# Gated mix of an S4D convolution and a bilinear GLU: two of each inverse's four stores on GpSimd's queue, a refitted list schedule, and other warm-up work for TensorE

## The chip, the cores and the metric

The kernel runs on one core of one Trainium2 chip. The metric is the device time of one execution in microseconds, as the median of several runs: 584.83 us before the change (three runs, 584.66 to 585.61).

## The reference

Two branches see the same tokens `u` (2048 x 512), and a gate mixes them:

```python
x = A_u
g = _sigmoid((x * gate_w).sum(-1, keepdims=True))
a = _A_ref(x, ...)   # S4D: y = irfft(rfft(u, 4096) * rfft(K, 4096)) + u * D_skip
b = _B_ref(x, ...)   # bilinear GLU: ((x W_gate) * (x W_up)) W_down
return g * a + (1 - g) * b
```

K is the convolution kernel of each of the 512 channels, 2 Re sum over 128 states n of C exp(A dt pos). The GLU is 1792 wide. All is float32.

## The kernel before

**GLU.** The width 1792 is 14 tiles of 128, in four groups (3, 3, 4 and 4 tiles); each group goes over four chunks of 512 tokens. For a tile and a chunk TensorE computes `pg` (gate) and `pu` (up), ScalarE copies `pg` to `h`, VectorE multiplies by `pu`, and the product is split into a high and a low part, `hh` (ScalarE) and `hl` (VectorE), in float32r. All operands of the large matmuls are split in this way, so each product is three matmuls of 128x128 by 128x512: `pg<-xs,wlo` once and `pg<-xs,whi` twice, likewise for `pu`, and `y<-dhi,hl`, `y<-dlo,hh`, `y<-dhi,hh` for the down product. These 2016 matmuls fill most of TensorE's time. At the end of a group ScalarE scales `y` by 1-g into `acc` (three buffers, line 719 on). Group 0 stores `acc` to `out`; the other groups add it there by an accumulating DMA on GpSimd's queue (`out<-acc`).

**Convolution.** It is done as transforms of length 4096 by small matmuls, in four quarters q of 128 channels. VectorE and ScalarE build tables `v` and `x` for 16 blocks of 32 channels; a **k-block** (`kgen`, line 1164) sums over the states with 64 matmuls of 32x64, `k<-v,x`, whose result goes to `kt`. Four blocks make a quarter: `k_first` transforms it and stores it to DRAM as `sk_d`; the tokens' first stage (`u_part`) goes to `su_d` by GpSimd's queue. Then, for each of four parts T of a quarter (`transforms`, line 1459): `m_load` loads `in` from `su_d` and `sk_d` on GpSimd's queue; the **second stage** (`m_second`, line 1278) is 16 matmuls of 32x512, `k<-in,w2s`, evicted by ScalarE to `ev`; `m_product` multiplies the two spectra on VectorE into `y`. After two parts the **inverse** (`m_inverse`, line 1335) is 64 matmuls of 64x128, `k<-y,w3s`. ScalarE evicts its four banks to two tiles `ts`, and four stores (`y_d<-ts`, 256 KB each, lines 1364 to 1375), two for each tile, one for each p, write them to `y_d`. So there are eight inverses and 32 stores. `m_last` reads `y_d` back on SyncE's queue (`in<-y_d`, `x<-y_d`), does the last 16 or 32 matmuls `k<-in,w_t`, applies the gate and adds to `out` by GpSimd's queue. The tiles of `y_d` and `sk_d` in the last quarter are called `ri`, `e`, `x` and `v`, after the tables whose place they take.

**What sets the order.** No line of the code is executed where it stands. Each operation is recorded as a task by `add(engine, us, fn, r, w, rank, after, dma, hold, rows, count, slack)`, and `Work.plan` (line 355) is a list scheduler: it models the time of every task from the costs given, always takes the task that can start first, and among equals the one of lower rank. `Work.run` then issues the tasks in that order, which is fixed for each engine (`InOrder`, line 116; so all instructions of the engines bear line 124). The model's numbers are part of the kernel:

- `us` is the time on the engine, `dma` the size of a transfer in KB at `DMA_RATE`. `Bus` (line 170) serves two queues of transfers, the hardware one and GpSimd's, in proportion to `WEIGHT`. `SENT` is the time from an issue to the transfer's begin, `LANDED` that from its end to the signal, and `SURE` what a reader leaves on top of it.
- `slack` is added to the time at which a task's inputs are ready. `EASE` adds (slack, rank, lateness) to tasks named by engine, tiles and time.
- `fetched` (line 328) holds a task of TensorE back until the instructions are likely to be there: with blocks of 256 instructions that are asked for when TensorE passes a place one block and `LEAD` ahead, `FETCH` us later, and `BEHIND` times as much more as transfers then wait on the bus. `count` is the number of instructions of a task: 256 for a k-block and for an inverse, 64 for a second stage.

**First work.** `first_loads` (line 577) has VectorE write zeros into a tile, and TensorE multiply them (lines 594 to 603) until the first operands have come.

The evictions before the stores are one `act` task for each bank, and the store takes the tile as its input:

```python
for j in range(4):
    st, m = sts[j // 2], j % 2
    evict(q, j, 0.6, ..., [banks[j]], [(st, m)])
```

Of the kernel before, what the change touches and what calls it, by code (L numbers as in the profile page):

```python
# [10 lines left out]
F32 = mybir.dt.float32  # L11
# [3 lines left out]
ALU = mybir.AluOpType  # L15
# [3 lines left out]
P = 128  # L19
# [150 lines left out]
class Bus:  # L170

    WEIGHT = 1.0, 1.58

# [31 lines left out]
class Work:  # L205
# [14 lines left out]

    BLOCK, FIRST, LEAD, FETCH = 256, 193, 64, 5.0
    TABLE = 1.3
    ROOM = {"dve": 0.6, "act": 0.4}
    BEYOND = 60
    BEHIND = 1.05

    EASE = {
        "act:k/e:0.4": (3, 0, 0),
        "act:k/in:0.32": (0.0, 1, 0),
        "act:pb/x:0.31": (0.0, 0, -60),  # L230
        "act:raw/whi:0.62": (0.0, 0, -60),
        "act:t/rt:0.77": (0.0, 0, -200),
        "dve:ev/y:0.6": (3, 0, 0),
        "dve:k/kt:0.42": (0.0, -1, 0),
        "dve:m/v:1.09": (0.0, 0, -20),
        "pool:ts:0.95": (2, 0, 0),
        "sp:in:0.42": (0.0, 1, 0),
        "sp:ri:0.42": (2, 0, 0),
        "sp:w3s/w2s/v:1.3": (0.0, 1, 0),
    }  # L240
    DMA_RATE = 0.33

    SENT = {"sp": 1.15, "act": 1.15, "pool": 1.98}
    LANDED = {"sp": 1.79, "act": 1.79, "pool": 1.5}
    SURE = 2

# [32 lines left out]
    def ready(self, task, d):  # L279

        if d.engine == task.engine == "pe":
            return d.end
        if d.dma and d.start > 20.0 and task.engine in ("pe", "act", "dve"):
            return d.end + self.SURE
        return d.end + self.LAG.get(task.engine, 0.03) + (self.PE_LAG if d.engine == "pe" else 0.0)
# [164 lines left out]
def gated_mix_kernel(  # L450
# [84 lines left out]
    def load(key, src, rank=0):  # L535
        if key in raws:
            return
        t = raws[key] = new("glu", "raw", [P, D], bufs=2)
        add("sp", 0.42, lambda: sp.dma_start(t.t, src), w=[t], dma=256, rank=rank)

# [20 lines left out]
    def rest(hi, lo, src, n):  # L561

        add("act", 0.19 + 0.43 * n, lambda: act.mul(lo.t, hi.t.bitcast(F32), -1.0), r=[hi], w=[lo], rank=0)
        add("pool", 0.95, lambda: pool_q.dma_start(lo.t, src, accum_op=ALU.add), w=[lo], dma=485 * n if n > 1 else 414, rank=0)

# [11 lines left out]
    def first_loads():  # L577
        in_y = lambda shape: new("mid", "y", shape, bufs=2)
        in_ev = lambda shape: new("mid", "ev", shape, bufs=2)
        in_in = lambda shape: new("mid", "in", shape, bufs=2)  # L580
        xsrc = lambda kt: xT[P * kt : P * kt + P, :D]
        w0 = raws["w0"] = in_ev([P, 2, D])
        xt = [load_two(lambda k, n=n: ("x", 0, 0, 2 * n + k), in_y, None, False) for n in range(2)]
        wsrc = wts[0][:, : 2 * D].rearrange("p (k d) -> p k d", k=2)
        for kt in range(KT):

            t, k, ks = xt[kt // 2], kt % 2, slice(P * kt, P * kt + P)
            add("sp", 0.42, lambda t=t, k=k, kt=kt: sp.dma_start(t.t[:, k], xsrc(kt)), w=[(t, k)], dma=256, rank=-1)
# [56 lines left out]
    def tokens(gi, ci, kt):  # L645

        x = xs[kt] = new("glu", "xs", [P, 2, D], F32R, 5)
        if gi:
            add("sp", 0.42, lambda: sp.dma_start(x.t.bitcast(F32), xs_d[ci, kt]), r=[(m_xs, (ci, kt))], w=[x], dma=422, rank=0)
# [3 lines left out]
        add("sp", 0.42, lambda: sp.dma_start(xs_d[ci, kt], x.t.bitcast(F32)), r=[x], w=[(m_xs, (ci, kt))], dma=462, rank=2, after=16.0 + kt if ci == 0 else 0.0)  # L653

# [64 lines left out]
    def evacuate(gi, ci, r, y):  # L719
# [10 lines left out]
        if final:  # L730
            ending.append((r, acc))
        elif gi == 0:
            add("sp", 0.42, lambda: sp.dma_start(ov[:, t, :], acc.t), r=[acc], w=[(m_out, t)], dma=134)
# [82 lines left out]
    def u_part(t):  # L816
        ut = inp([P, 4, D])
        rs = slice(4 * t, 4 * t + 4)
        add("sp", 0.42, lambda: sp.dma_start(ut.t, uv[:, rs, :]), w=[ut], dma=929, after=6.0 + (U_STEP + 1.0) * t)

# [30 lines left out]
        def first(s):  # L851
# [20 lines left out]
            for q in range(KT):  # L872
# [4 lines left out]
                    ),  # L877
                    r=[st], w=[(m_su, (q, n0))], dma=227,
                )
# [92 lines left out]
    def parameters(bs):  # L972
# [7 lines left out]

        add("sp", 0.84, fn, r=m_par, w=[pb], dma=173 * n)
        real = lambda: pb.t[:, 0, :n, 0]
# [178 lines left out]
    def k_block(b, x, v):  # L1161
# [31 lines left out]
    def k_first(q, kt):  # L1193
# [5 lines left out]
        for h in range(2):  # L1199
# [20 lines left out]
            for n0, n, st in sts:  # L1220
                for c in range(4):
# [11 lines left out]
                    ),  # L1233
                    r=[st], w=[(m_sk, (q, m)) for m in range(n0, n0 + n, 8)], dma=41 * n,
                )
# [11 lines left out]

    def w_load(tag, shape, src, kb=327):
        t = new("mid", tag, shape, bufs=2)
        add("sp", 0.42, lambda: sp.dma_start(t.t, src), w=[t], dma=kb, after=150.0)  # L1250
        return t

    def m_load(q, T):
# [11 lines left out]
        for w, (src, m) in enumerate(((su_d, m_su), (sk_d, m_sk))):  # L1265
# [5 lines left out]
                ),  # L1271
                r=[(m, (q, n0)) for n0 in range(0, 32, 8 if w else 4)], w=[(t, (T, w))], dma=655 if w else 585,
            )
# [61 lines left out]
    def m_inverse(q, T0, ys, ws):  # L1335
# [49 lines left out]
    def m_last(q, gs):  # L1385
# [30 lines left out]
        for g, t, n0, n in pieces:  # L1416
# [30 lines left out]
            if n == 1 and n0 == LAST % 2:  # L1447
# [7 lines left out]
                lambda rs=rs, flat=flat: pool_q.dma_start(ov[:, rs[0] : rs[-1] + 1, cs], flat(), accum_op=ALU.add),  # L1455
                r=[*parts, *((m_out, r) for r in rs)], dma=119 * len(rs), rows=rs,
            )
# [113 lines left out]
```

## Time and profile before

| | |
|---|---|
| time, median of 3 runs | 584.83 us (584.66 to 585.61) |
| the profiled execution | 589.44 us, span 587.5 us |
| mean granted clock of TensorE | 0.994 |
| instructions | 14848 |
| DMA | 136.28 MB, 232 GB/s over the span |
| q1, hardware queues (SyncE, ScalarE) | 43.0% of 16 engines' span |
| q0, GpSimd's queue | 39.3% |

One execution was profiled. PE is TensorE's matmuls, PEld its weight loads, which run beside them; DVE is VectorE, ACT ScalarE, POOL GpSimd, SP SyncE. Tiles stand as output <- inputs. In the groups and waits "<-" ahead of a name stands for what ended the idle time; "issue" is time in which the engine waited for nothing that the profile shows. A line of the timeline is start, length, engine, line, operation, tiles, shapes and count, with the wait ahead of it in brackets. A line of the windows is the stretch, its length, the busy time of PE, PEld, DVE, ACT and POOL with their instructions, the granted clock of TensorE (1.00 is full), the busy share of the 16 DMA engines, and GB/s.

### The profile page before, as it was taken

Reading aid. Unit: us, or ns where it says so; the run is one execution under the profiler, and the core shown is the slowest. Engines: PE = TensorE matmul, PEld = TensorE weight load, DVE = VectorE, ACT = ScalarE, POOL = GpSimd, SP = SyncE. Lnnn points to the kernel's source line nnn. Section 1 sums busy time; section 2 is a strip of 40 time slices with the busy share of each in tenths; the row PEclk is TensorE's granted clock in tenths of the full one; section 3 lists DMA queues with packets and bytes.
Section 4 is the critical chain, followed back from the end, with each engine's and each line's share of the span. In section 5 each row is a group of like instructions: output and inputs, shape, how many; then the busy total and the mean of one; then the engine's idle time right before and its main releaser. Section 6 shows DMA issues by size and latency. Waiting matters only on the chain.

```text
span 587.5 us, 14848 instructions
## 1 busy us (share of the span) xinstructions
PE 576.0 (98%) x5996; PEld 435.4 (74%) x5996; DVE 511.7 (87%) x812; ACT 399.1 (68%) x891; POOL 113.3 (19%) x159
## 2 busy tenths in 40 slices
PE   8999999989999999999999999999999999999995
PEld 5777777877887777888767678877778777777774
DVE  5999999977999999999999899996899998346745
ACT  4459978987568779975987585699858553333351
POOL 0003222410201141311122301133221004012011
PEclk9999999998999999999999999999999999999998
DMA  8999959996845798999879958889968259799686
GB/s 282 386 331 351 396 211 362 261 253 161 201 147 88 252 266 190 199 260 285 188 229 241 213 136 299 201 212 195 260 162 246 38 150 280 267 331 239 197 188 125
DMA packets 71687, 136.28 MB, mean 232 GB/s; under 512 B 6852, under 2 KB 35780, under 8 KB 69188
## 3 DMA queue, kind: packets, MB, share of 16 engines
q1 hardware_dynamic: 47668, 87.10, 43.0%
q0 software_dynamic: 23392, 47.98, 39.3%
q8 instruction: 47, 0.77, 0.5%
q10 hardware_dynamic: 560, 0.26, 0.2%
q14 instruction: 20, 0.16, 0.1%
HBM read 80.27 MB, written 55.05 MB: 230 GB/s over the span
## 4 chain that ended last, share of the span: by engine, by line
PE 91%; issue 4%; DMA 2%; POOL 1%; ACT 1%; DVE 1%; DVEq 0%; POOLq 0%; ACTq 0%
PE pg L124 26%; PE pu L124 26%; PE y L124 24%; PE k L124 15%; DMA in<-sk_d 1%; DMA y<-in_xT 1%; DMA sk_d<-ev 1%; POOL out L124 1%; POOL in L124 0%; ACT ev L124 0%; DVE y L124 0%; ACT h L124 0%; ACT xs L124 0%; DVE hl L124 0%; DVE dlo L124 0%
## 5 line engine op out<-in xcount | busy, mean ns | idle before, releaser
L124 PE MATMUL pu<-xs,whi 128*128 128x512 f32 x448 | 140.3, 395 | 0.0
L124 PE MATMUL pg<-xs,whi 128*128 128x512 f32 x448 | 139.4, 392 | 0.5 <-ACT whi L124 0.5
L124 PEld LDWEIGHTS pg<-xs,whi 128*128 128x128 f32 x448 | 84.7, 189 | 19.3 <-ACT whi L124 2.1
L124 PEld LDWEIGHTS pu<-xs,whi 128*128 128x128 f32 x448 | 85.4, 191 | 17.4
L124 PE MATMUL pg<-xs,wlo 128*128 128x512 f32 x224 | 90.6, 405 | 0.1
L124 PE MATMUL y<-dhi,hl 128*128 128x512 f32 x224 | 89.6, 400 | 0.6 <-DVE hl L124 0.6
L124 PE MATMUL pu<-xs,wlo 128*128 128x512 f32 x224 | 90.2, 403 | 0.0
L124 PE MATMUL y<-dlo,hh 128*128 128x512 f32 x224 | 87.4, 390 | 0.0
L124 PE MATMUL y<-dhi,hh 128*128 128x512 f32 x224 | 87.2, 389 | 0.0
L124 POOL DMA_DIRECT2D out<-acc x44 | 38.6, 955 | 167.9 <-ACT acc L124 160.0
L124 ACT COPY ev<-k 128x512 f32<-128x512 f32 x112 | 59.3, 598 | 16.5 <-PE k L124 16.5
L124 ACT CAST hh<-h 128x512 fp32r<-128x512 f32 x56 | 34.8, 622 | 45.8 <-DVE h L124 45.6
L124 DVE TENSOR_TENSOR h<-pu,h 128x512 f32<-128x512 f32 x56 | 38.6, 689 | 30.2 <-PE pu L124 29.7
L124 PEld LDWEIGHTS pu<-xs,wlo 128*128 128x128 f32 x224 | 42.6, 190 | 20.1 <-issue 11.4
L124 ACT ACTIVATE acc<-y,ngate 128x512 f32<-128x512 f32 x62 | 41.7, 685 | 22.7 <-PE y L124 20.5
L124 PEld LDWEIGHTS pg<-xs,wlo 128*128 128x128 f32 x224 | 42.4, 189 | 19.8 <-issue 9.5
L124 ACT COPY h<-pg 128x512 f32<-128x512 f32 x56 | 32.8, 586 | 34.9 <-PE pg L124 33.1
L124 PEld LDWEIGHTS y<-dhi,hl 128*128 128x128 f32 x224 | 42.0, 188 | 19.3 <-issue 7.7
L124 PEld LDWEIGHTS y<-dhi,hh 128*128 128x128 f32 x224 | 42.1, 188 | 9.0
L124 PEld LDWEIGHTS y<-dlo,hh 128*128 128x128 f32 x224 | 42.1, 188 | 7.8
L124 DVE TENSOR_TENSOR hl<-h,hh 128x512 fp32r<-128x512 f32 x56 | 38.4, 685 | 3.2 <-ACT hh L124 3.1
L124 PEld LDWEIGHTS k<-v,x 128*32 128x32 f32 x2048 | 29.4, 110 | 7.6 <-issue 7.2
(130 smaller groups left out, 962.9 us busy)
## 6 DMA issues: line engine op xcount, KB each, us to landing
xs<-xs_d SPq DMA_DIRECT2D x36, 512.0 KB, 6.7
out<-acc POOLq DMA_DIRECT2D x44, 256.0 KB, 6.1
raw<-in_wts SPq DMA_DIRECT2D x33, 256.0 KB, 4.5
xs_d<-xs SPq DMA_DIRECT2D x16, 512.0 KB, 7.6
su_d<-ev POOLq DMA_DIRECT2D x32, 256.0 KB, 7.2
y_d<-ts SPq DMA_DIRECT2D x28, 256.0 KB, 5.8
in<-su_d POOLq DMA_DIRECT2D x12, 512.0 KB, 6.6
sk_d<-ev SPq DMA_DIRECT2D x6, 1024.0 KB, 4.9
```

Of the source, the lines that this page charges most:

```text
L124: got = getattr(self.engine, name)(*args, **kw)
```

## The change

- In `m_inverse` the stores of p = 1, two of the four of each inverse, are issued on GpSimd's queue; only the last inverse (q = 3, T0 = 2) keeps all four on SyncE's. So 14 stores move: SyncE issues 237 DMAs instead of 251, GpSimd 148 instead of 134. A store there is planned with 0.55 us.
- The numbers of the plan are others: `WEIGHT` of GpSimd's queue 1.14 instead of 1.58, `SENT`, `LANDED`, the `dma` sizes of nearly all transfers, `FETCH` 5.5 instead of 5.0 and `BEHIND` 0.8 instead of 1.05, most entries of `EASE`, and `SURE`, which was 2 for three engines and is 3 for TensorE now. A k-block has a slack of 2.0 instead of 1.0.
- In `first_loads` zeros are written to 128x128 instead of 128x512, and TensorE multiplies them three times instead of twice: by 512, 512 and 128 columns, which are the same 128 read again.

```diff
 class Bus:
-    WEIGHT = 1.0, 1.58
+    WEIGHT = 1.0, 1.14
...
-    BLOCK, FIRST, LEAD, FETCH = 256, 193, 64, 5.0
+    BLOCK, FIRST, LEAD, FETCH = 256, 193, 64, 5.5
...
-    BEHIND = 1.05
+    BEHIND = 0.8
...
     EASE = {
-        "act:k/e:0.4": (3, 0, 0),
...
+        "pe:kt/k/ts:2.13": (1, 0, 0),
...
-    SENT = {"sp": 1.15, "act": 1.15, "pool": 1.98}
-    LANDED = {"sp": 1.79, "act": 1.79, "pool": 1.5}
-    SURE = 2
+    SENT = {"sp": 1.39, "act": 1.39, "pool": 1.79}
+    LANDED = {"sp": 1.46, "act": 1.46, "pool": 1.66}
+    SURE = {"pe": 3, "act": 2, "dve": 2}
...
-        if d.dma and d.start > 20.0 and task.engine in ("pe", "act", "dve"):
-            return d.end + self.SURE
+        if d.dma and d.start > 20.0 and task.engine in self.SURE:
+            return d.end + self.SURE[task.engine]
...
-        add("dve", 0.2, lambda: dve.memset(zero.t, 0.0), w=[zero], rank=-1)
+        add("dve", 0.06, lambda: dve.memset(zero.t[:, :P], 0.0), w=[zero], rank=-1)
         def warm():
-            for _ in range(2):
-                pe.matmul(scratch.t, zero.t[:, :P], zero.t, start=True, stop=True)
-        add("pe", 3.4, warm, r=[zero], w=[scratch], rank=-1, count=8)
+            w = zero.t[:, :P]
+            for n in (4, 4, 1):
+                to = scratch.t[:, : n * P].rearrange("p (n d) -> p n d", d=P)
+                rhs = w.unsqueeze(1).broadcast_to([P, n, P])
+                pe.matmul(to, w, rhs, start=True, stop=True)
+        add("pe", 3.85, warm, r=[zero], w=[scratch], rank=-1, count=12)
...
-                r=[acc, (m_out, t)], dma=431, rows=[t],
+                r=[acc, (m_out, t)], dma=442, rows=[t],
...
-        add("pe", 2.05, kgen, r=[x, v], w=[pk], rank=0, hold=[kt], count=256, slack=1.0)
+        add("pe", 2.05, kgen, r=[x, v], w=[pk], rank=0, hold=[kt], count=256, slack=2.0)
...
                 b0 = 32 * (T0 + p) + 16 * h
+                e, us, queue = ("pool", 0.55, pool_q) if p and (q < KT - 1 or not T0) else ("sp", 0.42, sp)
                 add(
-                    "sp", 0.42,
-                    lambda b0=b0, st=st, p=p: sp.dma_start(
+                    e, us,
+                    lambda b0=b0, st=st, p=p, queue=queue: queue.dma_start(
...
-                    r=[st], w=[(m_y, (q, T0 + h, p))], dma=303,
+                    r=[st], w=[(m_y, (q, T0 + h, p))], dma=311,
```

The new numbers give another order on every engine. Three places follow, each row an instruction with its tiles, shape and, where it repeats, its count.

The first place is on TensorE, a little past the middle of its order, before: down products of the GLU stand ahead of these rows, and the second stage of part T = 2 of quarter q = 1 (`k<-in,w2s`) stands among the GLU's matmuls.

```order
L124 MATMUL pg<-xs,wlo 128x512
L124 MATMUL pg<-xs,whi 128x512 x2
L124 MATMUL k<-in,w2s 32x512 x16
L124 MATMUL pu<-xs,wlo 128x512
L124 MATMUL pu<-xs,whi 128x512 x2
```

The same place now: behind the same down products stands the inverse of that quarter's first two parts (`k<-y,w3s`).

```order
L124 MATMUL y<-dlo,hh 128x512
L124 MATMUL y<-dhi,hh 128x512
L124 MATMUL k<-y,w3s 64x128 x64
L124 MATMUL pg<-xs,wlo 128x512
L124 MATMUL pg<-xs,whi 128x512 x2
```

The inverse, which came later, moved ahead of the second stage. Behind it now come 24 matmuls of the GLU, a k-block and 15 more, and only then the second stage.

The second place is on TensorE too, at the first quarter's inverse of parts 0 and 1, at about 230 us in the trace of before. Before, a k-block, 15 matmuls of the GLU, and then a second stage:

```order
L124 MATMUL k<-v,x 32x64 x64
L124 MATMUL pg<-xs,wlo 128x512
L124 MATMUL pg<-xs,whi 128x512 x2
L124 MATMUL pg<-xs,wlo 128x512
L124 MATMUL pg<-xs,whi 128x512 x2
L124 MATMUL pu<-xs,wlo 128x512
L124 MATMUL pu<-xs,whi 128x512 x2
L124 MATMUL pu<-xs,wlo 128x512
L124 MATMUL pu<-xs,whi 128x512 x2
L124 MATMUL pu<-xs,wlo 128x512
L124 MATMUL pu<-xs,whi 128x512 x2
L124 MATMUL k<-in,w2s 32x512 x16
```

Now the same k-block, 12 matmuls of the GLU, and the inverse:

```order
L124 MATMUL k<-v,x 32x64 x64
L124 MATMUL pu<-xs,wlo 128x512
L124 MATMUL pu<-xs,whi 128x512 x2
L124 MATMUL pu<-xs,wlo 128x512
L124 MATMUL pu<-xs,whi 128x512 x2
L124 MATMUL pu<-xs,wlo 128x512
L124 MATMUL pu<-xs,whi 128x512 x2
L124 MATMUL y<-dhi,hl 128x512
L124 MATMUL y<-dlo,hh 128x512
L124 MATMUL y<-dhi,hh 128x512
L124 MATMUL k<-y,w3s 64x128 x64
```

A block of 64 small matmuls (256 instructions in the plan) stands where one of 16 (64 instructions) stood, and three matmuls of the GLU closer to the k-block.

The third place is on GpSimd's queue, a piece of the difference near its middle (- before, + now), with the adds of the GLU (`out<-acc`) and the stores of inverses (`y_d<-ts`):

```order
 L124 DMA in<-sk_d 128x8x128
-L124 DMA out<-acc 128x512 x8
+L124 DMA out<-acc 128x512 x3
+L124 DMA y_d<-ts 64x8x128 x2
+L124 DMA out<-acc 128x512
+L124 DMA y_d<-ts 64x8x128 x2
+L124 DMA out<-acc 128x512 x4
 L124 DMA wlo<-in_wts 128x1024
```

Four stores, two of each of two inverses, stand between the eight adds.

More of the change, by code (lines that the diff above doesn't have):

```diff
@@ L224 @@
     BEYOND = 60
-    BEHIND = 1.05
+    BEHIND = 0.8
     EASE = {
-        "act:k/e:0.4": (3, 0, 0),
-        "act:k/in:0.32": (0.0, 1, 0),
-        "act:pb/x:0.31": (0.0, 0, -60),
+        "act:k/in:0.59": (0.0, 0, -200),
         "act:raw/whi:0.62": (0.0, 0, -60),
         "act:t/rt:0.77": (0.0, 0, -200),
+        "act:v/sq:1.17": (0.0, 0, 20),
         "dve:ev/y:0.6": (3, 0, 0),
[L234 to L238, printed above, removed]
+        "dve:k/in:0.42": (0.0, 1, 0),
+        "pe:kt/k/ts:2.13": (1, 0, 0),
         "sp:w3s/w2s/v:1.3": (0.0, 1, 0),
@@ L538, in load @@
         t = raws[key] = new("glu", "raw", [P, D], bufs=2)
-        add("sp", 0.42, lambda: sp.dma_start(t.t, src), w=[t], dma=256, rank=rank)
+        add("sp", 0.42, lambda: sp.dma_start(t.t, src), w=[t], dma=300, rank=rank)
     def split(hi, lo, s, key):
@@ L563, in rest @@
         add("act", 0.19 + 0.43 * n, lambda: act.mul(lo.t, hi.t.bitcast(F32), -1.0), r=[hi], w=[lo], rank=0)
-        add("pool", 0.95, lambda: pool_q.dma_start(lo.t, src, accum_op=ALU.add), w=[lo], dma=485 * n if n > 1 else 414, rank=0)
+        add("pool", 0.95, lambda: pool_q.dma_start(lo.t, src, accum_op=ALU.add), w=[lo], dma=385 * n if n > 1 else 364, rank=0)
     def load_two(key, tile_of, src, one=True):
@@ L648, in tokens @@
         if gi:
-            add("sp", 0.42, lambda: sp.dma_start(x.t.bitcast(F32), xs_d[ci, kt]), r=[(m_xs, (ci, kt))], w=[x], dma=422, rank=0)
+            add("sp", 0.42, lambda: sp.dma_start(x.t.bitcast(F32), xs_d[ci, kt]), r=[(m_xs, (ci, kt))], w=[x], dma=442, rank=0)
             return
@@ L652, in tokens @@
         split(x, x, (0, 1), ("x", gi, ci, kt))
-        add("sp", 0.42, lambda: sp.dma_start(xs_d[ci, kt], x.t.bitcast(F32)), r=[x], w=[(m_xs, (ci, kt))], dma=462, rank=2, after=16.0 + kt if ci == 0 else 0.0)
+        add("sp", 0.42, lambda: sp.dma_start(xs_d[ci, kt], x.t.bitcast(F32)), r=[x], w=[(m_xs, (ci, kt))], dma=426, rank=2, after=16.0 + kt if ci == 0 else 0.0)
     def ahead(ci):
@@ L732, in evacuate @@
         elif gi == 0:
-            add("sp", 0.42, lambda: sp.dma_start(ov[:, t, :], acc.t), r=[acc], w=[(m_out, t)], dma=134)
+            add("sp", 0.42, lambda: sp.dma_start(ov[:, t, :], acc.t), r=[acc], w=[(m_out, t)], dma=213)
         else:
@@ L818, in u_part @@
         rs = slice(4 * t, 4 * t + 4)
-        add("sp", 0.42, lambda: sp.dma_start(ut.t, uv[:, rs, :]), w=[ut], dma=929, after=6.0 + (U_STEP + 1.0) * t)
+        add("sp", 0.42, lambda: sp.dma_start(ut.t, uv[:, rs, :]), w=[ut], dma=840, after=6.0 + (U_STEP + 1.0) * t)
         def score_of(j):
@@ L877, in first @@
                     ),
-                    r=[st], w=[(m_su, (q, n0))], dma=227,
+                    r=[st], w=[(m_su, (q, n0))], dma=250,
                 )
@@ L979, in fn @@
                 sp.dma_start(pb.t[:, k, :n], par_d[:, k, bs[0] : bs[0] + n])
-        add("sp", 0.84, fn, r=m_par, w=[pb], dma=173 * n)
+        add("sp", 0.84, fn, r=m_par, w=[pb], dma=140 * n)
         real = lambda: pb.t[:, 0, :n, 0]
@@ L1233, in k_first @@
                     ),
-                    r=[st], w=[(m_sk, (q, m)) for m in range(n0, n0 + n, 8)], dma=41 * n,
+                    r=[st], w=[(m_sk, (q, m)) for m in range(n0, n0 + n, 8)], dma=50 * n,
                 )
@@ L1246, in gated_mix_kernel, with w_load @@
     m_w4 = work.memory()
-    def w_load(tag, shape, src, kb=327):
+    def w_load(tag, shape, src, kb=388):
         t = new("mid", tag, shape, bufs=2)
@@ L1271, in m_load @@
                 ),
-                r=[(m, (q, n0)) for n0 in range(0, 32, 8 if w else 4)], w=[(t, (T, w))], dma=655 if w else 585,
+                r=[(m, (q, n0)) for n0 in range(0, 32, 8 if w else 4)], w=[(t, (T, w))], dma=584 if w else 551,
             )
@@ L1455, in m_last @@
                 lambda rs=rs, flat=flat: pool_q.dma_start(ov[:, rs[0] : rs[-1] + 1, cs], flat(), accum_op=ALU.add),
-                r=[*parts, *((m_out, r) for r in rs)], dma=119 * len(rs), rows=rs,
+                r=[*parts, *((m_out, r) for r in rs)], dma=132 * len(rs), rows=rs,
             )
```

## Prediction

> **What bounds the kernel now.** I read the page first: the engines' shares and the chain that ended last.
>
> ```profile
> PE 576.0 (98%) x5996; PEld 435.4 (74%) x5996; DVE 511.7 (87%) x812; ACT 399.1 (68%) x891; POOL 113.3 (19%) x159
> PE 91%; issue 4%; DMA 2%; POOL 1%; ACT 1%; DVE 1%; DVEq 0%; POOLq 0%; ACTq 0%
> 340.47 2.73 PE pu L124 x12
> ```
>
> TensorE is on the chain for 91%, and once it runs it takes 2.73 us for 12 matmuls of the GLU, 0.227 us each (third line, a piece of the chain in order of time: start, length). The change neither adds nor removes a matmul behind the first work, so it can only win what TensorE waits. Hence the waits of PE alone, next:
>
> ```profile
> PE k L124 <- issue: 1.8, 1, 1.8
> PE k L124 <- DVE acc L124: 1.5, 1, 1.5
> PE k L124 <- DMA in<-sk_d: 1.2, 1, 1.2
> PE y L124 <- DVE hl L124: 0.6, 1, 0.6
> PE pg L124 <- ACT whi L124: 0.5, 1, 0.5
> ```
>
> Five waits of 5.6 us together, each once (us in total, times, longest). There is little to win and no floor under a loss. The timeline around the two that lie in mid-kernel:
>
> ```profile
> 126.68 0.63 DVE L124 TENSOR_TENSOR v<-v,sq 128x256 f32<-128x256 f32 x1
> 128.62 1.98 PE L124 MATMUL k<-v,x 128*32 128x64 f32 x125
> 132.36 0.30 PE L124 MATMUL k<-v,x 128*32 128x64 f32 x3 [1.76 <-issue]
> ...
> 326.36 0.92 POOL L124 DMA_DIRECT2D in<-sk_d  x1 [6.94 <-issue]
> 331.52 1.15 PE L124 MATMUL k<-in,w2s 32*32 32x512 f32 x32 [1.16 <-DMA in<-sk_d]
> ```
>
> The first is inside one k-block (64 small matmuls, 128 records): 125 records run, then TensorE has nothing to wait for in the profile ("issue") for 1.76 us, then the last three. I read that as instructions that had not arrived; such a block uses up in 2 us, with 128 loads and 128 matmuls, as many instructions as the GLU in 29 (a load and a matmul in 0.227 us). The second is a second-stage block whose input was asked for 5.2 us before (326.36 to 331.52). What the first wait did to the clock stands in the windows:
>
> ```profile
> 130.24:133.65 3.41, 1.65 (x33) 1.21 (x22) 2.66 (x5) 1.79 (x10) 0.50 (x1) 1.00 0.77 151
> 133.65:137.07 3.42, 3.42 (x10) 2.64 (x9) 1.36 (x3) 2.61 (x7) 0.00 (x0) 0.50 0.47 141
> ```
>
> Behind the stretch with the wait, 3.42 us run at a granted clock of 0.50 (third value from the end): 1.71 us more are lost. So this one event costs 3.47 us, the largest of the trace.
>
> **The change part by part.** The sum is made against the profiled execution, 589.44 us, of which 587.5 are the span. The median of the timed runs is 584.83, 4.61 us less: the timed executions lack something, and the 3.47 us event is the only single loss of nearly that size. I can't see whether they have it, so I count it there at half.
>
> *Second stage later, inverse earlier* (the first place of the order). The block that waited at 331.52 stood 9 GLU matmuls behind the down products; now an inverse, a k-block and 39 GLU matmuls stand between: 2.0 + 1.9 + 30 x 0.227 = 10.7 us later. Its load has that much more time, and the wait of 1.16 us goes. What is late next is the inverse that took its place: it needs the products of VectorE, which here end at 325.18 + 2.42 = 327.60.
>
> ```profile
> 325.18 2.42 DVE L124 TENSOR_TENSOR y<-y,ev 128x512 f32<-128x512 f32 x4
> 328.16 0.39 PE L124 MATMUL pg<-xs,wlo 128*128 128x512 f32 x1
> ```
>
> TensorE comes to that place at 328.16 (today's first matmul behind the down products), 0.56 us later. It fits, barely. Term: -1.2, between -1.2 and +0.5.
>
> *k-blocks with 2 us of slack instead of 1.* v was ready at 126.68 + 0.63 = 127.31 and the block began at 128.62: 1.31 us, about the planned one. A microsecond more lets the instructions behind the block be asked for that much sooner, if the wait is what holds them back. The 1.76 us become 0.8, and as the waits of 1.16 and 0.56 us left the clock at 1.00 I take it that the half window goes too: -1.0 - 1.7 = -2.7 in the profiled execution, half of it, -1.35, in the timed ones. Bounds: 0 and -3.5.
>
> *Two of the four stores on GpSimd.* Fourteen stores move. An issue costs GpSimd between 0.56 and 0.96 us, 14 x 0.56 = 7.8 us of an engine that is busy for 19%; SyncE gets 14 times 0.66 back.
>
> ```profile
> L124 POOL DMA_DIRECT2D out<-acc x44 | 38.6, 955 | 167.9 <-ACT acc L124 160.0 <-ACT kt L124 7.1 <-ACT ev L124 0.8
> L124 POOL DMA_DIRECT2D su_d<-ev x32 | 17.4, 556 | 80.9 <-ACT ev L124 80.9
> su_d<-ev POOLq DMA_DIRECT2D x32, 256.0 KB, 7.2
> y_d<-ts SPq DMA_DIRECT2D x28, 256.0 KB, 5.8
> L124 SPq DMA_DIRECT2D y_d<-ts x28: 580/655/4049, 245.6 to 541.1; - x28
> L124 SPq DMA_DIRECT2D in<-y_d x12: 490/497/606, 260.1 to 528.0; - x12
> 298.98 1.95 PE L124 MATMUL k<-in,w_t 64*32 64x512 f32 x32
> ```
>
> Stores of the same size land after 7.2 us from GpSimd and 5.8 from SyncE, so the last of a set may come 1.4 us later or, with two queues issuing at once, 2 x 0.66 earlier. Who waits is SyncE's load of y_d; TensorE uses the first of these from 298.98 on, 38.9 us after its issue at 260.1, and the last four stores of the kernel stay on SyncE. Behind a store on GpSimd's queue stand `out<-acc` adds; if the store waits for its evictions, they wait too, and ScalarE's evictions of y after three buffers. In the trace GpSimd itself waited for ScalarE 160.0 us before these adds, which is the cover. Term 0, between -0.6 and +1.4.
>
> *First work on fewer zeros.*
>
> ```profile
> 0.92 0.48 DVE L124 MEMSET acc<- 128x512 f32 x1 [0.92 <-PEq L1560]
> 1.39 0.17 DVE L124 MEMSET skip<- 128x128 f32 x1
> 1.46 3.78 PE L124 MATMUL k<-acc 128*128 128x512 f32 x4 [1.46 <-DVE acc L124]
> 5.75 1.22 PE L124 MATMUL pg<-xs,whi 128*128 128x512 f32 x2 [0.51 <-ACT whi L124]
> ...
> 8.47 1.05 PE L124 MATMUL pg<-xs,whi 128*128 128x512 f32 x2
> 9.76 1.05 PE L124 MATMUL pu<-xs,whi 128*128 128x512 f32 x2
> 10.93 0.63 PE L124 MATMUL pg<-xs,whi 128*128 128x512 f32 x2
> 11.62 0.62 PE L124 MATMUL pu<-xs,whi 128*128 128x512 f32 x2
> ...
> 28.32 0.50 PE L124 MATMUL y<-dhi,hl 128*128 128x512 f32 x1 [0.56 <-DVE hl L124]
> ```
>
> A memset of a quarter takes 0.17 instead of 0.48 us, so the zeros start 0.3 us sooner; the third matmul, a quarter of one, adds 2 x 0.21 at the same rate. They end 0.1 us later, still ahead of 5.75, which ScalarE's split sets. Up to about 10.8 three matmuls take 1.29 us (8.47 to 9.76), from 10.93 on 0.69: the clock doubles there. If the longer work brought that forward by one stretch of 3.4 us, TensorE would gain 1.7 us, but at 28.32 it waits for VectorE's hl already, and would wait longer by what it gained. Term 0, between -1.7 and 0. [...]
>
> *New order elsewhere.* The refitted numbers move rows on every engine. Near 230 us an inverse now follows a k-block after 12 GLU matmuls (the second place of the order), where a second-stage block of a quarter of its instructions followed after 15. The trace has such a pair, k-block at 471.25 and inverse at 476.11 with 12 matmuls between, and no wait in it:
>
> ```profile
> 471.25 1.92 PE k L124 x128
> 473.17 2.94 PE pg L124 x12
> 476.11 2.02 PE k L124 x125
> 220.00:240.00 20.00, 20.00 (x261) 14.50 (x260) 19.06 (x32) 19.17 (x48) 4.41 (x7) 1.00 0.82 191
> 460.00:480.00 20.00, 20.00 (x352) 15.52 (x352) 19.96 (x32) 10.98 (x23) 0.93 (x1) 1.00 0.18 46
> ```
>
> But there the DMA engines were busy for 0.18 (second value from the end), near 230 for 0.82, and for 0.77 where the k-block of 130 stopped. A new wait for instructions costs between 0 and the 3.47 us of that event; I take half of its bare wait, +0.9.
>
> Sums: profiled, 589.44 - 1.2 - 2.7 + 0.9 = 586.4. Timed, 584.83 - 1.2 - 1.35 + 0.9 = **583.2 us**.
>
> **The rivals.** *No change.* That is the case in which the change does not do what it says. The gains lie in two events of one execution; if the timed runs lack the first, 584.83 - 1.2 + 0.9 = 584.5 is left, and a second-stage or hl wait of 0.6 elsewhere makes it nothing. For it: the runs lie 4.61 us below the profile. Against: the 1.16 us wait is a plain DMA wait. Range 583.7 to 585.9.
>
> *Slower.* The inverse near 230 stops as the k-block at 130 did, because its instructions come through DMA engines that are busy for 0.82, and the clock halves behind it: 584.83 - 1.2 + 1.76 + 1.71 = 587.1. The pair decides from the point at which instructions take longer than the k-block and 12 matmuls, 1.9 + 2.7 = 4.6 us. For it: the two blocks need twice the instructions of the one that stopped. Against: the same pair ran freely at 471.
>
> [...]
>
> **How the numbers follow.** Forecast 0.36, range 582.3 to 583.6; more than forecast 0.06; no change 0.34; slower 0.24, 586.0 to 588. 0.2% are 1.17 us, about what a measurement of this kernel can tell from none. Faster 0.36 + 0.06 = 0.42, same 0.34, slower 0.24. The range goes from 581.3, which leaves out half of the low case, to 587.3, which leaves out half of the slow one: about 0.15 left out.
>
> **What would show it.** Right: no DMA wait at a second-stage block near 330; a bare wait under 1 us near 130 and the clock at 1.00 behind it; the first GLU matmul still at 5.7; no wait of PE on in<-y_d. Wrong: an "issue" wait inside a k-block or inverse at 228 to 236 with a stretch at 0.50 behind it; ScalarE's acc waiting for out<-acc and PE's y behind it; the clock at full speed before 8 us.

## The result, and the profile after

The changed kernel takes **592.09 us** (median of 17 runs, 586.7 to 596.39), the kernel before 585.6 in as many runs beside it (581.94 to 589.93). The ratio is 1.0078, 95% interval 1.0053 to 1.0103: slower by 0.8%. The ratio is that of the fast runs, which leaves out two of the changed kernel's 17 (595.51 and 596.39); the quotient of the two medians would be 1.011. The profiled execution after lies at its median (592.09, span 590.3); the one of before, 589.44, lies 3.84 above the median of its 17 runs, which matters below.

TensorE's waits after, as in the prediction (us in total, times, longest):

```profile
PE k L124 <- issue: 6.9, 2, 4.2
PE k L124 <- DVE acc L124: 1.1, 1, 1.1
PE y L124 <- DVE x L124: 0.7, 1, 0.7
PE y L124 <- DVE hl L124: 0.6, 1, 0.6
PE pg L124 <- ACT whi L124: 0.4, 1, 0.4
```

The wait for in<-sk_d is gone. Two waits for instructions, 6.9 us, stand where there was one of 1.8 ("issue": TensorE waited for nothing that the profile shows, which the prediction read as instructions that had not arrived). The timeline of TensorE and SyncE around them:

```profile
232.98 0.50 PE L124 MATMUL y<-dhi,hl 128*128 128x512 f32 x1 [0.70 <-DVE x L124]
...
254.32 1.15 SPq L124 DMA_DIRECT2D in<-y_d  x2
256.44 1.99 PE L124 MATMUL k<-v,x 128*32 128x64 f32 x127
262.58 0.32 PE L124 MATMUL k<-v,x 128*32 128x64 f32 x1 [4.15 <-issue]
...
331.22 2.10 PE L124 MATMUL k<-y,w3s 32*64 32x128 f32 x128
338.90 1.99 PE L124 MATMUL k<-v,x 128*32 128x64 f32 x126
343.68 0.30 PE L124 MATMUL k<-v,x 128*32 128x64 f32 x2 [2.79 <-issue]
```

Both "issue" waits are in k-blocks that stop one or two records before their end. The first block follows two loads of y_d, 1 MB together, that SyncE issued 2 us earlier; the second follows the inverse that the new order put ahead of the second stage. The windows there (granted clock third from the end, then the DMA engines' busy share):

```profile
256.00:260.00 4.00, 2.43 (x130) 1.92 (x128) 3.93 (x9) 2.86 (x4) 0.10 (x1) 1.00 0.85 264
260.00:264.00 4.00, 1.42 (x4) 1.11 (x5) 0.72 (x2) 1.06 (x4) 0.00 (x0) 0.61 0.32 60
264.00:268.00 4.00, 4.00 (x12) 3.08 (x11) 3.48 (x5) 1.48 (x5) 0.00 (x0) 0.54 0.02 4
331.00:337.00 6.00, 6.00 (x147) 4.96 (x145) 5.90 (x13) 3.42 (x6) 4.74 (x6) 1.00 0.97 274
337.00:340.00 3.00, 3.00 (x87) 2.41 (x89) 2.99 (x4) 1.72 (x8) 0.00 (x0) 1.00 1.10 262
```

Behind the first wait the clock halves: the trace's clock records have it from 260.88 to 267.71, of which TensorE worked from 262.58 on, so 5.13 / 2 = 2.6 us more. That the waits are for instructions shows in the records of the instruction queue, 47 packets of 16384 bytes in each of the two traces. At these waits TensorE goes on 1.4 to 1.6 us after one has come (times in us):

```
kernel   packet starts   takes   ends     TensorE goes on at
before   129.84          0.90    130.74   132.36
after    230.54          0.90    231.44   232.98
after    260.05          1.11    261.16   262.58
after    341.30          0.94    342.24   343.68
```

The row at 232.98 is the wait that the profile puts down to DVE x. The tile x is no input of that matmul and was done at 232.55 (it started at 231.47 and took 1.08), and the distance to the packet is the same as in the other rows. So I count its 0.70 us as a wait for instructions too; the experiments below give a second reason.

The start and the end are better than before. The first wait for hl, and the last piece of TensorE in the chain (before, then after):

```profile
26.03 0.50 PE L124 MATMUL y<-dhi,hl 128*128 128x512 f32 x1 [0.56 <-DVE hl L124]
```

```profile
575.85 5.70 PE y L124 x24
```

```profile
580.97 5.75 PE y L124 x24
```

It comes at 26.03 instead of 28.32: -2.3. Behind TensorE's last matmul 587.5 - 581.55 = 5.95 us were left, now 590.3 - 586.72 = 3.58: -2.4. The sum over the two profiles: waits for instructions +5.9 (6.94 + 0.70 - 1.76), half clock in mid-kernel +0.9 (2.6 - 1.7), the wait for in<-sk_d -1.2, start -2.3, end -2.4: +0.9 of the +2.8 between the spans. The other 1.9 us lie in TensorE's busy time (1.5) and in its gaps of under 0.15 us (0.4), and I can't name them one by one.

### The profile page after: what moved, and what is told of

The parts are those of the page before. It is cut to its first block, busy times and chain, and to the rows that moved or that the text cites. A ratio compares the mean times of both kernels' runs of the same rounds, so it can differ in the third digit from the quotient of the medians.

```text
span 590.3 us, 14859 instructions
## 1 busy us (share of the span) xinstructions
PE 576.6 (98%) x5998; PEld 434.7 (74%) x5998; DVE 512.7 (87%) x812; ACT 400.9 (68%) x891; POOL 123.9 (21%) x173
## 4 chain that ended last, share of the span: by engine, by line
PE 89%; DVE 4%; DMA 3%; issue 2%; ACT 1%; SPq 0%; DVEq 0%; ACTq 0%
PE y L124 25%; PE pu L124 24%; PE pg L124 24%; PE k L124 16%; DMA raw<-in_wts 2%; DVE x L124 1%; DMA y<-in_xT 1%; DVE y L124 1%; DVE hl L124 1%; DVE wlo L124 0%; DVE h L124 0%; ACT acc L124 0%; DVE dlo L124 0%; DVE small L124 0%; SPq L124 0%
## 5 line engine op out<-in xcount | busy, mean ns | idle before, releaser
L124 PE MATMUL pu<-xs,whi 128*128 128x512 f32 x448 | 138.7, 391 | 0.0
L124 PE MATMUL k<-v,x 128*32 128x64 f32 x2048 | 32.5, 220 | 6.9 <-issue 6.9
```

The source lines that it names most:

```text
L124: got = getattr(self.engine, name)(*args, **kw)
```

## The experiments

All ratios are to the kernel before, run beside each on the same chip, with 95% intervals. Theory O says that the order costs the time, Q that the queue does, S that the few added instructions do; L and C are two causes of the late packets, P and D the rivals of these, and F says that two of the plan's numbers brought the late packets.

### One part alone: first work, queue, order

*New first work in the kernel before.* The edit is the part of the change in `first_loads` with the plan's costs left as they were:

```diff
-        add("dve", 0.2, lambda: dve.memset(zero.t, 0.0), w=[zero], rank=-1)
+        add("dve", 0.2, lambda: dve.memset(zero.t[:, :P], 0.0), w=[zero], rank=-1)
         def warm():
-            for _ in range(2):
-                pe.matmul(scratch.t, zero.t[:, :P], zero.t, start=True, stop=True)
+            w = zero.t[:, :P]
+            for n in (4, 4, 1):
...
```

> The kernel before, its order and its queues, with the new first work alone (zeros 128x128, matmuls of 512, 512 and 128 columns; the plan's numbers untouched). Theory O (the refitted order makes instructions arrive late; the first work is a gain): the first wait for hl ends near 26 us instead of 28.3, full clock from about 6 us, and the time falls by about 2 us, from 585.6 to 583.5 (ratio 0.996). Theory S (the few more TensorE instructions shift where the blocks of 256 instructions begin, and that makes them late): new waits of 2 to 4 us inside k-blocks, near 588 to 590 (1.005 or more).

Measured: 583.31 us, ratio 0.9972 (0.9954 to 0.9991). The first wait for hl ends at 26.40, and no k-block has a wait. Theory O by the time; the new waits of theory S did not come. Where the gain comes from is less clear: the wait near 130 is gone too, and a profile of the old first work that starts as well (the next run, hl at 26.30) has a span only 0.9 us longer, 582.5 against 581.6, with a wait of 1.09 near 130.

*Stores on GpSimd's queue in the kernel before's order.*

```diff
-                    lambda b0=b0, st=st, p=p: sp.dma_start(
+                    lambda b0=b0, st=st, p=p: (pool_q if p and (q < KT - 1 or not T0) else sp).dma_start(
```

> The kernel before, with the order of TensorE, VectorE and ScalarE as before and the same 14 stores issued on GpSimd's queue. Theory O: no difference, 585.6 (ratio 0.998 to 1.002). Theory Q (stores on GpSimd's queue hold up the instruction packets, or GpSimd's adds behind them): 588 to 590, with longer waits inside k-blocks or before out<-acc and y.

Measured: 585.99 us, ratio 1.0009 (0.9992 to 1.0027): no cost and no gain of the queue can be told. The wait near 130 is there with 1.09 us:

```profile
129.56 0.30 PE L124 MATMUL k<-v,x 128*32 128x64 f32 x3 [1.09 <-issue]
```

*The changed kernel with all stores on SyncE.*

```diff
-                    lambda b0=b0, st=st, p=p, queue=queue: queue.dma_start(
+                    lambda b0=b0, st=st, p=p: sp.dma_start(
```

> The changed kernel with its order on TensorE, VectorE and ScalarE and its first work, but all stores of the inverses issued on SyncE. Theory O: as the changed kernel, about 591 (ratio 1.005 to 1.012), with the waits in the k-blocks near 258 and 340. Theory Q: near 584 to 586 (0.997 to 1.000), those waits gone.

Measured: 589.34 us, ratio 1.0077 (1.0051 to 1.0103), the same as with the stores moved, and the same two waits, with one of 0.96 at 131.74 beside them. Theory Q is out.

```profile
263.27 0.31 PE L124 MATMUL k<-v,x 128*32 128x64 f32 x1 [2.88 <-issue]
343.23 0.30 PE L124 MATMUL k<-v,x 128*32 128x64 f32 x3 [2.62 <-issue]
```

*The changed kernel with the old first work.* The edit is the first one the other way round.

> The changed kernel with the first work of before (two matmuls of 512 columns on 128x512 zeros), the order as changed. Theory O: the gain at the start is lost, 2 us more than the changed kernel, about 593 to 594 (ratio 1.013), first wait for hl near 28.3. Theory S: the block boundaries fall back, the waits near 258 and 340 change or go, 586 to 588 (1.002).

Measured: 589.94 us, ratio 1.0081 (1.0055 to 1.0108). The loss stays; that the first work was to cost 2 us here does not show, since the intervals are wider than that against the changed kernel. The waits are worth a look:

```profile
263.41 1.22 PE L124 MATMUL pu<-xs,whi 128*128 128x512 f32 x2 [2.59 <-issue]
342.97 0.50 PE L124 MATMUL pg<-xs,wlo 128*128 128x512 f32 x1 [2.51 <-issue]
```

The old first work has one matmul less, which is four instructions in the plan's count. In the changed kernel the first k-block stops after 127 of 128 records (254 of its 256 instructions) and the second after 126 (252). Here both run through, and TensorE stops at instruction 258 (the whole block and one matmul of the GLU) and at 256: four further on, both times. So the wait is tied to a place in the stream of instructions, not to data, and theory S is out here as well: the places shift, the loss stays. The traces bear this out when everything that TensorE executes is counted (weight loads, matmuls, semaphore instructions): in both kernels the stops come after 4545 and 6593 instructions, and all 22 "issue" waits of the 14 profiles come after 193 + 256 n, as 4545 = 193 + 256 x 17, and the one of before near 130 after 1729 = 193 + 256 x 6. The wait at 232.98 in the changed kernel, put down to DVE x, comes after 4033 = 193 + 256 x 15.

### What makes the packets late

For these the list that `plan` returns is changed by hand before it is run, so that one thing moves and all else stays in its order.

*The loads of y_d later.* In `run`, the two loads go behind the next task of SyncE:

```diff
-        for t in self.plan():
+        order = self.plan()
+        held = [t for t in order if t.name == ("y_d load", 0, 0)]
+        order = [t for t in order if t not in held]
+        at = next(n for n, t in enumerate(order) if t.engine == "sp" and t.start > held[-1].start) + 1
+        order[at:at] = held
+        for t in order:
             t.fn()
```

> The changed kernel with one thing moved on SyncE's queue: the two loads in<-y_d that are issued at 254.3 and 254.9 come behind the next xs<-xs_d, so some 15 us later. Theory L (these loads fill the DMA engines from 255 to 260, and the instruction packet of the k-block lies behind them): the wait of 4.15 us in the k-block near 258 falls below 1 us and the half clock behind it goes; 3.5 to 6 us less than the changed kernel, 586 to 588 (ratio 1.001 to 1.004); the wait near 340 stays. Theory P (the order leaves too little time between the small-matmul blocks, whatever the transfers): the wait stays at 3 to 4 us, ratio 1.007 to 1.009.

Measured: 587.48 us, ratio 1.0026 (1.0007 to 1.0044), where the changed kernel has 1.0078 (1.0053 to 1.0103): 3 us less. The loads are issued at 263.4 instead of 254.3, by the view of their tile (durations in ns, least, median and longest; first and last start):

```profile
L124 SPq DMA_DIRECT2D in<-y_d x2: 517/528/539, 263.4 to 264.0; - x2
```

The k-block starts as in the changed kernel and now runs through (timeline); the second wait stays:

```profile
256.40 1.99 PE L124 MATMUL k<-v,x 128*32 128x64 f32 x128
337.99 0.30 PE L124 MATMUL k<-v,x 128*32 128x64 f32 x2 [3.21 <-issue]
```

The packet came at 255.36, in the changed kernel at 260.05, with the k-block at 256.4 in both: 4.7 us of delay that go with the two loads. The wait goes with them, and 3 of the 3.5 to 6 us that were expected. Theory L is shown. The other runs agree: counted from one and the same instruction, 320 ahead of the stop, this packet starts 8.8 to 12.0 us later in the five profiles of this order that have the loads ahead of it, and 6.1 to 7.4 us later in the three that have them moved.

*The k-block near 340 later.* It moves past the GLU matmuls up to the next small block, with what depends on it:

```diff
+        block = [t for t in order if t.name == "k-block"][9]
+        i = order.index(block)
+        j = next(n for n, t in enumerate(order) if n > i and t.engine == "pe" and not 6 < t.count < 7)
+        moved, kept = [block], []
+        for t in order[i + 1 : j]:
+            (moved if t.deps & set(moved) else kept).append(t)
+        order[i:j] = kept + moved
```

> The changed kernel with one thing moved on TensorE: the k-block that waits near 340, 24 GLU matmuls behind the inverse that moved ahead, comes 15 GLU matmuls (3.4 us) later. Theory C (inverse and k-block use up 512 instructions within 8 us, faster than the packets come): the wait of 2.79 us near 340 goes, 2 to 3 us less than the changed kernel, near 588.5 (ratio 1.003 to 1.005); the wait near 258 stays. Theory D (the packet is asked for only when the k-block is near, so the wait goes with the block): a wait of 2 us or more stays, ratio 1.007 to 1.009.

Measured: 590.71 us, ratio 1.0079 (1.0051 to 1.0106): no gain that can be told, the time that theory D had. But the profile has no wait for instructions near 340. It has one for the k-block's evictions, which now come right ahead of the second stage and hold up its banks:

```profile
263.95 0.31 PE L124 MATMUL k<-v,x 128*32 128x64 f32 x1 [3.49 <-issue]
348.11 1.13 PE L124 MATMUL k<-in,w2s 32*32 32x512 f32 x26 [1.16 <-DVE kt L124]
```

By the profile theory C; the time is the one of D, and nothing of the 2 to 3 us that C had promised. The next two runs ask again.

*Both moves.*

> Both moves together in the changed kernel. Theories L and C: no wait over 1 us inside a k-block in mid-kernel; what is left of the change is its gain of the 1.16 us second-stage wait and some of the first work, so 583 to 584.5 (ratio 0.995 to 0.998), below the kernel before. If other places of the new order wait too: 586 or more (ratio over 1.001).

Measured: 585.77 us, ratio 0.9996 (0.9976 to 1.0015). No wait for instructions is left, and the whole loss is gone: the second move is worth 0.3% beside the first, though the intervals overlap. But it is no better than before, where 583 to 584.5 was expected. A wait of 2.00 us for the evictions stands near 340, and the clock halves for 3.4 us behind it:

```profile
340.81 1.13 PE L124 MATMUL k<-in,w2s 32*32 32x512 f32 x26 [2.00 <-DVE kt L124]
```

*Both moves, the k-block 9 matmuls later instead of 15* (`j` is the third task of TensorE behind it).

> As the run with both moves in the changed kernel, but the k-block near 340 comes only 9 GLU matmuls (2.04 us) later instead of 15, so that 6 stand between it and the second stage, which there waited 2.00 us for the k-block's evictions. Theory C: the wait for instructions is 2.79 less 2.04, so under 1 us, and the wait for the evictions falls below 1 us; 1 to 2 us less than with 15, 584 to 585 (ratio 0.994 to 0.999). If the clock still halves there or the waits add up as before, 585.8 (ratio 1.000).

Measured: 584.93 us, ratio 1.0002 (0.998 to 1.0025). The wait for instructions is 0.54 us, close to 2.79 - 2.04 = 0.75 (against the 3.21 us with the loads alone moved it fell by more, 2.67), and the one for evictions is gone:

```profile
338.77 0.41 PE L124 MATMUL k<-v,x 128*32 128x64 f32 x11 [0.54 <-issue]
```

So the packet does not move along with the block. Its own records say the same: in all seven profiles with this inverse ahead of the block it starts 9.0 to 10.5 us after the inverse does, whether the block follows 24, 33 or 39 matmuls behind (five of them, times in us):

```
kernel                              inverse   packet    after
after (24 matmuls)                  331.22    341.30    10.1
loads of y_d later (24)             325.05    335.59    10.5
both moves, 9 matmuls later (33)    326.59    336.58    10.0
k-block later (39)                  332.83    343.00    10.2
both moves (39)                     324.71    333.72     9.0
```

Theory C, and D is out. But the evictions' wait is gone as well and a gain over the kernel before still doesn't show, so that wait was not what held it back; this profile has a wait of 1.43 us near 130, where the changed kernel's had none.

### The numbers of the plan, one at a time

*The changed kernel with FETCH 5.0 and BEHIND 1.05*, as before:

```diff
-    BLOCK, FIRST, LEAD, FETCH = 256, 193, 64, 5.5
+    BLOCK, FIRST, LEAD, FETCH = 256, 193, 64, 5.0
...
-    BEHIND = 0.8
+    BEHIND = 1.05
```

> The changed kernel planned with FETCH 5.0 and BEHIND 1.05 as before, all other new numbers kept. TensorE's order is then as changed up to 330 us, and there the second stage comes ahead of k-block and inverse again, as before. Theory F (these two numbers let the plan put the inverse so close to the k-block): the wait near 340 goes, the wait near 258 stays with its half clock: 2 to 3 us less than the changed kernel, near 588.5 (ratio 1.003 to 1.006). If the wait near 340 stays or another takes its place, other numbers of the refit set it: ratio 1.007 to 1.010.

Measured: 598.46 us, ratio 1.0209 (1.0184 to 1.0234), far off either theory. Near 340 the wait is gone, as F had it (0.32 us), and near 258 it is 1.58:

```profile
259.30 0.24 PE L124 MATMUL k<-v,x 128*32 128x64 f32 x1 [1.58 <-issue]
334.83 0.75 PE L124 MATMUL k<-v,x 128*32 128x64 f32 x35 [0.32 <-issue]
```

The loss is at the other end, in the chain's last steps:

```profile
573.05 5.73 PE y L124 x24
578.79 1.10 PE k L124 x16
582.14 0.98 issue
583.12 2.01 DVE x L124 x5
585.13 2.92 DVE kt L124 x7
```

The last transform of the convolution now comes behind the last down products instead of among them, and VectorE's work on it and the stores behind end the kernel at 594.6, 14 us after TensorE (6 us in the kernel before).

*The kernel before with slack 2.0 for the k-blocks, and nothing else.*

```diff
-        add("pe", 2.05, kgen, ..., count=256, slack=1.0)
+        add("pe", 2.05, kgen, ..., count=256, slack=2.0)
```

> The kernel before, planned with a slack of 2.0 for the k-blocks and nothing else changed: one part of the change alone. The plan moves other blocks for it. My step of the prediction (more slack, less waiting for instructions): 583.5 to 585 (ratio 0.996 to 0.999), no wait near 130. Theory O (any new order brings blocks of instructions and loads together elsewhere, and its cost is not foreseen by the number that was changed): a wait of over 1.5 us in another block, ratio 1.002 to 1.010.

Measured: 590.98 us, ratio 1.01 (1.006 to 1.014). The wait near 130 is gone, as the prediction's step had it; another of 2.16 us stands in a k-block near 262:

```profile
263.66 0.42 PE L124 MATMUL k<-v,x 128*32 128x64 f32 x13 [2.16 <-issue]
```

The end is late here too, 11.2 us after TensorE, by the chain:

```profile
575.08 2.96 PE y L124 x12
579.57 2.01 DVE x L124 x5
581.58 2.92 DVE kt L124 x7
```

*The kernel before with FETCH 5.5 and BEHIND 0.8, and nothing else.*

> The kernel before, planned with FETCH 5.5 and BEHIND 0.8 and nothing else changed. Behind a busy bus the plan then reckons with 9.5 us instead of 10.25. Theory F (these two numbers bring the late instructions): waits of over 1.5 us in blocks near 230 to 340, ratio 1.003 to 1.010. If the other numbers do it: 585 to 586.5 (ratio 0.998 to 1.002).

Measured: 592.02 us, ratio 1.0107 (1.0075 to 1.0138), with two waits, behind each of which the clock halves for 3.4 us by the clock records:

```profile
130.44 0.30 PE L124 MATMUL k<-v,x 128*32 128x64 f32 x3 [1.93 <-issue]
265.25 1.22 PE L124 MATMUL pu<-xs,whi 128*128 128x512 f32 x2 [2.93 <-issue]
```

Its chain ends in the same way, 9.7 us after TensorE:

```profile
581.57 2.00 DVE x L124 x5
583.58 2.92 DVE kt L124 x7
```

All three plans with one or two numbers changed cost 1.0% to 2.1% against the kernel before, and all three lose at the end of the kernel, which none of the theories had foreseen. That speaks for theory O, but F is not out. With FETCH and BEHIND of before the wait near 340 shrank to 0.32 us, and with the new ones in the kernel before a wait of 2.93 us came at 265, both as F had it; only the times missed, 1.0209 by far and 1.0107 by little. Which number of the refit brings which of the changed kernel's two waits stays open, since every change of one number draws a new order.

### A version that beats both

*The kernel before with the new first work, and the second stage that waited near 331 moved past 6 matmuls of the GLU* by the same kind of edit as for the k-block.

> The kernel before with the new first work, and the second stage that waited at 331 us for in<-sk_d moved 6 GLU matmuls (1.36 us) later on TensorE; nothing else is moved. The wait (1.16 us in the profile of before, 0.62 with the new first work) goes and nothing is late in its place: 0.6 to 1.2 us less than with the first work alone, 582.5 (ratio 0.994 to 0.997). If the second stage's evictions then hold up the k-block behind it: no gain, ratio 0.997 to 0.999.

Measured: **582.87 us**, ratio 0.9953 (0.9932 to 0.9975), the fastest of all, as expected. What TensorE still waits for lies in the first 28 us:

```profile
PE k L124 <- DVE acc L124: 1.1, 1, 1.1
PE y L124 <- DVE hl L124: 0.6, 1, 0.6
PE pg L124 <- ACT whi L124: 0.5, 1, 0.5
```

## Why the prediction was wrong, point by point

The forecast was 583.2 us, a gain; the changed kernel is 0.8% slower, which makes 589.4 of 584.83.

- **New order elsewhere, +0.9: the term that failed.** In the profile the waits that the new order brings are 4.15 + 2.6 (half clock) + 2.79 + 0.70 = 10.2 us. The two large ones make up the loss: with the loads of y_d moved back the ratio falls from 1.0078 to 1.0026, with the k-block moved too to 0.9996. The mechanism was the one of the rival *Slower* (instructions that come late through busy DMA engines, here a packet at 260.05 instead of 255.36, with the engines busy for 0.85 from 256 to 260, and the clock that halves, from 260.88 to 267.71), but the place hardly: near 230 the k-block and the inverse ran through, and only 0.70 us were lost a little behind them. I had priced one place where two blocks of TensorE came close, and had not followed what the order moves on SyncE's queue: the loads of y_d went from 260.1 to 254.3, ahead of a k-block's packet. And it was more than one event, while 587.1 was priced with one: the loss lies beyond that case's 586 to 588 too.
- **Second stage later, inverse earlier, -1.2: half right.** The wait went, and moved by hand it brings the kernel from 0.9972 to 0.9953, near what was expected, though the intervals overlap. I asked whether the inverse's own data would be there, and they were. I didn't ask what comes behind it: a k-block 5.6 us later, with a wait of 2.79.
- **k-blocks with more slack, -1.35: wrong.** Alone the number makes the kernel 1.0% slower. The wait near 130 goes in that profile and in the changed kernel's, but two profiles of the changed kernel's order have it again, with 0.96 (all stores on SyncE) and 1.43 us (both moves, 9 matmuls). A slack in a list schedule doesn't add a microsecond to one block, it draws another order.
- **Stores on GpSimd, 0: right** as far as can be told, from both sides (1.0009 alone; 1.0077 with the new order and without them, 1.0078 with both).
- **First work, 0, between -1.7 and 0:** alone in the kernel before it brings 0.28% of 585.08 = 1.6 us, the low end, but that the start brings it isn't shown, since that profile lacks the wait near 130 as well. In the changed kernel the gain can't be told from nothing. Where the clock is full early, the start gains 2 us with the old first work too (the first wait for hl ends at 26.30 and 26.31 in two profiles, at 28.32 in the one of before): see the clock, below. The range's low end, 581.3, and the chance of 0.06 for more than the forecast lean on 1.7 us that this work would gain by an earlier full clock. No run shows that it does: with it the clock was full from 4.88 (after) or 10.25 (k-block later), with the old one from 5.67 (FETCH and BEHIND new) or 10.77 (before).
- **The end of the kernel, not looked at:** -2.4 us in the profile, and up to 8 us the other way in other plans.
- **The profile against the timed runs.** I put the gap of 4.61 us down to the event near 130, with 3.47. Some 2 us more of this profile were its start, at half clock up to 10.8. Two profiles of TensorE's same order with full clock from 5.8 (new first work) and 5.7 (stores on GpSimd) have spans of 581.6 and 582.5. And counting the event "at half" was too much: of 66 timed runs of the kernel before beside the experiments 9 have the profile's mean clock of 0.994, with 586.8 to 589.7 us, and all others 0.996 or more, so most lack the half clock near 130.

Of the signs named beforehand, the one near 330 and the one near 130 came out as for *right*, and the full clock before 8 us (from 4.88) as for *wrong*; none of them looked at 256 to 268 or at 340, where the loss is.

The case *no change* and the forecast both rested on the waits of before, which were all seen. What was not seen is that a forecast for a redrawn plan needs the waits that the new order makes. The trace of before had the price of one, 3.47 us; the two new ones cost 6.75 and 2.79.

## What to carry to other kernels

A number in a list scheduler's model doesn't buy what it is named for; it draws a new order. Four new orders here cost 0.8% to 2.1%, part of it at places that no number named, such as the kernel's end. Moves by hand took away the waits that they aimed at; by the ratio, the time that was worked out came in two of five such runs (the loads of y_d, and the second stage with the new first work). When the order of a kernel with dense blocks of small instructions changes, look at each block and at what is issued on every DMA queue in the 5 us ahead of it, and at the last 20 us, before counting the waits that go.

## What the runs showed of the hardware

**The granted clock in these traces.** The clock records of before and after change at points that lie whole multiples of 3.413 us apart (36, 37 and 168 of these behind the first record in before, 75, 77 and 172 in after), at another phase in each of the two (first record at 10.77 and 4.88 us). In the 14 profiles the clock first became full at 4.3 to 7.5 us (nine) or at 9.9 to 10.8 (five, the kernel before among them). In the stretch of 3.413 us up to that point TensorE was idle for 0.00 to 0.43 us in the nine; in the five a stretch with 0.50 to 0.68 us of idle time lies one ahead of it. (Ahead of the first record the windows view says 1.00, though in the trace of before three matmuls take 1.29 us up to 10.8 and 0.69 behind.)

```
full from   idle in the stretch before    kernel
4.88        0.00                          after
5.67        0.43                          before, FETCH and BEHIND new
10.25       0.50 (one stretch earlier)    after, k-block later
10.77       0.51 (one stretch earlier)    before
```

The pause ahead of the first real matmul was 0.22 to 0.84 us, and its length alone doesn't tell the two apart: 0.54 (FETCH and BEHIND new) and 0.84 (both moves) came with the early clock, 0.50 (k-block later) and 0.51 (before) with the late one. Both the old and the new first work had it either way, and the early clock is worth 2 us at the start. That the phase decides, by where in the stretches the pause falls, is my reading of these 14 profiles; it wasn't tried.

Once full, the clock halved ten times in mid-kernel, each time behind a wait of 1.76 us (before) to 4.15 us (after); it stayed full behind waits of 2.16 (slack 2.0), 2.51 (after, old first work) and 2.79 us (after, near 340), and behind all of 1.58 us or less. In the stretch of 3.413 us ahead of the fall TensorE was idle for 1.76 us (before) to 3.19 us. Two stretches with 1.91 (after, 339.38 to 342.80) and 2.02 us had no fall behind them, which I can't explain. Twice the clock stayed down for a second stretch, where the first one at half clock had 1.12 (k-block later) and 1.71 us (after, 260.88 to 264.29) of idle time itself.

**The instruction packets in these traces.** All 22 "issue" waits come after 193 + 256 n instructions of TensorE (1729 in before, 4545 and 6593 in after). With two loads of 512 KB issued 2 us ahead of a k-block its packet came at 260.05, with the loads moved back at 255.36: 4.7 us. That the packet near 341 waited for GpSimd's transfers (the DMA engines' share is 0.97 to 1.10 from 331 to 344) is read from the windows alone and wasn't tried.
